# K of the middle groups in one load, into two of three neighbouring pages

## The chip, the cores and the metric

The kernel runs on one core of a Trainium2 chip. Its five engines have instruction streams of their own and meet through semaphores: TensorE (PE in the profile, its weight loads PEld), VectorE (DVE), ScalarE (ACT), GpSimd (POOL) and SyncE (SP, which here issues every transfer). Transfers are carried by 16 DMA engines. The metric is the device time of one execution in microseconds (us); lower is better.

## The reference

One token is decoded through a gated mix of two branches: attention over a cache of 32,768 positions, and a small SwiGLU layer.

```python
B, Sq, D = 1, 1, 512
Hq, Hkv, Sk, Dh = 32, 8, 32768, 128          # 4 query heads share one of 8 groups of K and V
q = (x @ wq).reshape(B, Sq, Hq, Dh).transpose(0, 2, 1, 3)
scores = jnp.einsum("bhqd,bhkd->bhqk", q, k) * (Dh ** -0.5)
p = softmax(scores, axis=-1)
a = jnp.einsum("bhqk,bhkd->bhqd", p, v) ... @ wo
b = (silu(B_x @ w_gate) * (B_x @ w_up)) @ w_down           # F = 1792
g = sigmoid((A_x * gate_w).sum(-1, keepdims=True))
return g * a + (1 - g) * b
```

All tensors are bf16. K and V are 8.4 MB for each of the 8 groups, 134 MB together; all weights add some 14 MB.

## The kernel before, in words

A loop goes round G = 8 times, once for each group. A partition p holds 256 neighbouring positions of a group, 64 KB of K and as many of V. They lie in pages of 32 KB per partition (`page`, five of them): K's first 128 positions per partition (half b = 0) in page 0, its second 128 (b = 1) in page 1, V in pages 2 and 3. Page 3 first holds w_gate and w_up, page 4 first wq and at the end wo.

**K on TensorE** (`emit_k`, for each half). A half is cut into UPP = 8 units of 16 positions. `emit_fill` (L309) transposes a unit with eight fp32 transposes into one of two PSUM tiles `pst`; VectorE copies it to one of four tiles `ktT` (L635); `emit_scores` (L321) multiplies it with the queries, 16 small matmuls into the half's PSUM bank `ps_sc`. Unit u's fill stands ahead of the scores of unit u - 2 (LAG = 2). A fill waits until the copy two units back has emptied its PSUM tile, and scores wait for their own copy. Each half begins with two fills and ends with two scores, so the pipeline empties between the halves. After a half VectorE takes its maximum (L640).

**Softmax and V.** VectorE joins both maxima (L642), TensorE transposes (L343), VectorE reduces and makes a diagonal (L650, L654), and TensorE spreads it over the partitions (L347). ScalarE makes the bias of it (`nbias`, L516) and runs eight Exps (L523), four per half. Ahead of L516 it loads a function table in every turn. TensorE multiplies with V (L362), then sums the denominators (L374) and, from ScalarE's copy `acc` (L532), the parts of the output (L383). That is the end of a turn for TensorE.

**SP's queue.** SP issues wq, the two small rows, w_gate and w_up. Then, for each group in order, K's half 0, K's half 1, V; then w_down (`wd`) and wo in five pieces. A half of K waits until TensorE has filled the same half of the group before (`sem_fill`, `load_k`, L261 and L263); V waits until TensorE has finished V of the group before (`sem_v_free`, L269 and L274). Every K load has rows of 32 KB. V has one load with 64 KB rows, but for the last group, which is loaded in halves (L280). V's single load raises one semaphore; POOL waits on it and raises the second half's (L253 to L255).

**The end.** After the loop TensorE multiplies w_down (`emit_end`), VectorE makes the transposed output `O2` of all groups (L678, L685, L687), and TensorE multiplies with wo piece by piece as it lands (`emit_wo`: 24 rows as strips, L214, 8 rows as L225). ScalarE copies the strips' sum (L697), TensorE adds it, VectorE casts the result (L699) and SP stores it (L701).

On TensorE all of this is one instruction stream: group g + 1's fills stand behind group g's reduce, and the end behind group 7's reduce.

Of the kernel before, what the change touches and what calls it, by code (L numbers as in the profile page):

```python
# [5 lines left out]
ACT = mybir.ActivationFunctionType  # L6
ALU = mybir.AluOpType
AX = mybir.AxisListType
BF16 = mybir.dt.bfloat16
# [3 lines left out]
def bass_gated_mix__gqa_block_cached__swiglu_ffn__decode_kernel(  # L13
# [52 lines left out]
    assert RQ * HPG <= 32 and RQ * DH == 512  # L66
    assert QT == 2 and QN == 512 and F % (NSTRIP * FC) == 0 and FS <= 512

    PG_K = (0, 1)
    PG_V = 2  # L70
    PG_F = 3
    PG_X = 4
    NPG = 5

    with ExitStack() as es:
        def S_(name):
# [56 lines left out]
        def T(name, shape, dt):  # L133
            return es.enter_context(nc.sbuf_tensor(name, shape, dt))
# [25 lines left out]
        diag = T("diag", [HPG, HPG], FP32)  # L160
        nbias = T("nbias", [128, HPG], FP32)
        esum = T("esum", [128, NB, HPG], FP32)
        esum2 = T("esum2", [128, HPG], FP32)
        acc = T("acc", [128, RQ, DH], FP32)
        rS = T("rS", [128, HPG], FP32)
# [7 lines left out]
        def P(name, shape, dt):  # L173
            return es.enter_context(nc.psum_tensor(name, shape, dt))

        ps_sc = [P(f"ps_sc{i}", [128, 512], FP32) for i in range(NB)]
# [30 lines left out]
        wq_v = page[:, PG_X, 0 : KC * H * DH].rearrange("p (c n) -> p c n", c=KC)  # L207
# [40 lines left out]
        with nc.Block("main") as block:  # L248
            @block.gpsimd
            def _(pool):  # L250
                pool.memset(ones_f[:, :], 1.0).then_inc(sem_ones, 1)
                pool.memset(ones_bf[:, :], 1.0).then_inc(sem_ones, 1)
                for g in range(G - 1):  # L253
                    pool.wait_ge(sem_v[0], 16 * (g + 1))
                    pool.sem_inc(sem_v[1], 16)  # L255

            @block.sync
            def _(sp):
                def load_k(g, b):
                    if g:  # L260
                        sp.wait_ge(sem_fill, UPG * (g - 1) + UPP * (b + 1))  # L261
                    src = A_k_cache[0, g, :, :].rearrange("(p b r) d -> p b r d", b=NB, r=R)
                    sp.dma_start(  # L263
                        page[:, PG_K[b], :].rearrange("p (r d) -> p r d", d=DH), src[:, b, :, :]
                    ).then_inc(sem_k[b], 16)

                def load_v(g):
                    if g:
                        sp.wait_ge(sem_v_free, STEP * g)  # L269
                    else:  # L270
                        sp.wait_ge(sem_pe_h, 1)
                    src = A_v_cache[0, g, :, :].rearrange("(p b r) d -> p b r d", b=NB, r=R)
                    if g < G - 1:
                        sp.dma_start(  # L274
                            vpage.rearrange("p b r d -> p (b r d)"),
                            src.rearrange("p b r d -> p (b r d)"),
                        ).then_inc(sem_v[0], 16)
                    else:
                        for b in range(NB):
                            sp.dma_start(vpage[:, b, :, :], src[:, b, :, :]).then_inc(  # L280
                                sem_v[b], 16
                            )

                sp.dma_start(wq_v, A_wq.rearrange("(p c) n -> p c n", c=KC)).then_inc(sem_q, 16)
                sp.dma_start(x_row[0:1, :], A_x[0, :, :]).then_inc(sem_ld_x, 16)
                sp.dma_start(gw_row[0:1, :], gate_w.unsqueeze(0)).then_inc(sem_ld_g, 16)
                for w, src in enumerate((B_w_gate, B_w_up)):
                    sp.dma_start(  # L288
                        wgu[:, w, :, :], src.rearrange("(p c) f -> p c f", c=KC)
                    ).then_inc(sem_f, 16)  # L290
                for g in range(G):
                    for b in range(NB):
                        load_k(g, b)
                    load_v(g)
                sp.dma_start(  # L295
                    wd[:, :, :], B_w_down.rearrange("(p j) n -> p j n", j=FC)
                ).then_inc(sem_ld_wd, 16)
                src = A_wo.rearrange("(p j) n -> p j n", j=WOJ)
                for k, s in enumerate(sem_wo):
                    a, b = WO_CUTS[k], WO_CUTS[k + 1]  # L300
                    sp.dma_start(wo_v[:, a:b, :], src[:, a:b, :]).then_inc(s, 16)  # L301

            @block.tensor
            def _(pe):
                def emit_fill(b, u):
                    kv = page[:, PG_K[b], :].bitcast(FP32)
                    for k in range(RPU):
                        n = u * RPU + k
                        ins = pe.transpose(  # L309
                            pst[u % NST][:, k * 128 : (k + 1) * 128],  # L310
                            kv[:, n * 128 : (n + 1) * 128],
                            ident_f[:, :],
                        )
                    ins.then_inc(sem_fill, 1)
# [12 lines left out]
                            )  # L327
                    return ins

                def emit_k(i, b):  # L330
                    pe.wait_ge(sem_k[b], i + 16)
                    for u in range(UPP + LAG):
                        if u >= LAG:
                            pe.wait_ge(sem_cp, i + (UPP * b + u - LAG + 1))
                        if u < UPP:
                            emit_fill(b, u)
                        if u >= LAG:
                            ins = emit_scores(b, u - LAG)
                    ins.then_inc(sem_sc, UPP)

                def emit_max(i):
                    pe.wait_ge(sem_pm, i + STEP)
# [49 lines left out]
                def emit_start():  # L392
# [84 lines left out]
                    pe.wait_ge(sem_ps0, 1)  # L477

                    with pe.Fori(0, G * STEP, STEP) as i:
                        for b in range(NB):  # L480
                            emit_k(i, b)
                        emit_max(i)
                        emit_v(i)
                        emit_reduce(i)
# [20 lines left out]
            @block.scalar  # L505
            def _(act):
                act.wait_ge(sem_pe_g, 1)
                act.activation(
                    g_col[:, :], ps_m[:, M_G0 : M_G0 + 1], ACT.Sigmoid
                ).then_inc(sem_act_g, 1)  # L510
                act.wait_ge(sem_pe_h, 1)
                act.activation(sg, pst[1][:, 0:FS], ACT.Sigmoid).then_inc(sem_act_sg, 1)

                with act.Fori(0, G * STEP, STEP) as i:
                    act.wait_ge(sem_b, i + STEP)
                    act.activation(  # L516
                        nbias[:, :], ps_m[:, M_B0 : M_B0 + HPG], ACT.Copy, scale=-SCALE
                    ).then_inc(sem_nbias, STEP)
# [12 lines left out]
                    act.wait_ge(sem_v_free, i + STEP)  # L531
                    act.activation(part, ps_o[:, :], ACT.Copy).then_inc(sem_acc, STEP)  # L532

            @block.vector
            def _(dve):
# [93 lines left out]
                dve.tensor_copy(tT[:, :], ps_m[:, M_T0 : M_T0 + FC]).then_inc(sem_dve_tT, 1)  # L629

                with dve.Fori(0, G * STEP, STEP) as i:
                    for b in range(NB):
                        for u in range(UPP):
                            dve.wait_ge(sem_fill, i + (UPP * b + u + 1))
                            dve.tensor_copy(  # L635
                                ktT[:, u % NKT, :], pst[u % NST][:, :].bitcast(BF16)
                            ).then_inc(sem_cp, 1)
                        dve.wait_ge(sem_sc, i + UPP * (b + 1))
                        sc = ps_sc[b][:, :].rearrange("p (t h) -> p h t", h=HPG)
                        dve.tensor_reduce(pmaxf[:, b, :], sc, AX.X, ALU.max).then_inc(sem_d, 1)  # L640
# [93 lines left out]
```

## Time and profile before

| | |
|---|---|
| median of 3 runs | 351.64 us (351.43 to 351.78) |
| the profiled execution | 351.67 us, span 350.4 us |
| mean granted TensorE clock | 0.864 |
| TensorE busy | 254.6 us (73%) |
| weight loads | 209.2 us (60%) |
| VectorE busy | 192.1 us (55%) |
| ScalarE busy | 42.9 us (12%) |
| read from HBM | 148.11 MB, 423 GB/s over the span |

Busy time is the time in which an engine has an instruction running; it says nothing on whether anybody waits for it. In the groups of instructions a line gives the source line, the engine, the operation, output and inputs, and how often it ran. In the timeline the first two columns are the start and the length in us, and the brackets at the end give how long the engine had been idle and what ended that. SPq is SP's queue; its rows are the issues of transfers, not their duration. The waits list the engine and line, what it waited for, the sum in us, how often, and the longest.

### The profile page before, as it was taken

How to read it: one execution, taken by the hardware profiler on the slowest of the kernel's cores; microseconds unless marked ns; L12 is line 12 of the kernel's file. 1: busy time of each engine (PE TensorE's matmuls, PEld its weight loads, DVE VectorE, ACT ScalarE, POOL GpSimd, SP SyncE). 2: the span in 40 equal slices, each digit the busy share in tenths (PEclk: the TensorE clock that was granted, in tenths of full speed). 3: DMA queues.
4: the chain of work that ended last, by engine and by line, in shares of the span. 5: the costliest groups of instructions: out<-in, count | busy, mean ns of one | idle time of the engine just before them, and what ended most of it. 6: DMA issues, size and time to landing. Idle time of an engine off the chain costs nothing.

```text
span 350.4 us, 8660 instructions
## 1 busy us (share of the span) xinstructions
PE 254.6 (73%) x3871; PEld 209.2 (60%) x3871; DVE 192.1 (55%) x242; ACT 42.9 (12%) x156; POOL 0.4 (0%) x6
## 2 busy tenths in 40 slices
PE   1443986688857994898858993798768893798574
PEld 1113985288725984398726991498627891498431
DVE  4243986068803885068804892088705891198500
ACT  1000000400050002300050005000050005000130
POOL 0000000000000000000000000000000000000000
PEclk9965999699968997689969997889859995899878
DMA  8999999999989999999999999999999999999995
GB/s 337 408 451 419 477 443 384 423 430 456 464 385 417 456 426 430 423 464 434 434 404 419 464 449 400 423 449 434 434 419 419 464 434 415 423 426 434 420 423 205
DMA packets 4914, 148.21 MB, mean 423 GB/s; under 512 B 554, under 2 KB 556, under 8 KB 940
## 3 DMA queue, kind: packets, MB, share of 16 engines
q1 hardware_dynamic: 4908, 148.12, 98.4%
q8 instruction: 5, 0.08, 0.1%
q14 instruction: 1, 0.01, 0.0%
HBM read 148.11 MB, written 0.00 MB: 423 GB/s over the span
## 4 chain that ended last, share of the span: by engine, by line
DMA 69%; PE 25%; DVE 3%; SPq 1%; ACT 1%; issue 1%; DVEq 0%; ACTq 0%
DMA page<-in_A_k_cache_dram 56%; PE pst L309 18%; DMA page<-in_A_wo_dram 12%; PE ps_sc L321 5%; DVE ktT L635 2%; PE ps_o L362 2%; SPq L301 0%; ACT ET L523 0%; ACT L516 0%; SPq L288 0%; SPq L280 0%; DVE pmaxf L640 0%; PE ps_m L347 0%; SPq L295 0%; PE ps_sc L225 0%
## 5 line engine op out<-in xcount | busy, mean ns | idle before, releaser
L635 DVE COPY ktT<-pst 128x2048 bf16<-128x2048 bf16 x128 | 155.4, 1223 | 31.1 <-PE pst L309 23.4
L309 PE MATMUL pst<-ident_f,page 128*128 128x128 f32 x1024 | 140.5, 286 | 15.6 <-DMA page<-in_A_k_cache_dram 10.3
L309 PEld LDWEIGHTS pst<-ident_f,page 128*128 128x128 f32 x1024 | 115.9, 146 | 19.8 <-DMA page<-in_A_k_cache_dram 11.0
L321 PE MATMUL ps_sc<-qcur,ktT 128*128 128x8 bf16 x2048 | 67.8, 166 | 8.6 <-DVE ktT L635 8.6
L321 PEld LDWEIGHTS ps_sc<-qcur,ktT 128*128 128x128 bf16 x2048 | 66.7, 97 | 11.2 <-DVE ktT L635 10.0
L362 PE MATMUL ps_o<-page,ET 128*16 128x512 bf16 x512 | 43.6, 515 | 27.1 <-ACT ET L523 27.1
L362 PEld LDWEIGHTS ps_o<-page,ET 128*16 128x16 bf16 x512 | 15.8, 113 | 51.5 <-issue 36.4
L516 ACT ACT_TABLE_LOAD x8 | 10.3, 1283 | 239.0 <-PE ps_m L347 239.0
L658 DVE TENSOR_TENSOR esum<-esum 128x4 f32<-128x4 f32 x8 | 1.3, 164 | 42.7 <-ACT ET L523 42.7
L523 ACT ACTIVATE ET<-ps_sc,nbias 128x128 bf16<-128x128 f32 x64 | 23.9, 562 | 0.7
L662 DVE RECIPROCAL rS<-ps_sc 128x4 f32<-128x4 f32 x8 | 1.5, 182 | 34.2 <-PE ps_sc L374 34.2
L523 ACT ACTIVATION_READ_ACCUMULATOR ET<-ps_sc,nbias 128x1 f32 x64 | 18.6, 290 | 0.0
L640 DVE TENSOR_REDUCE pmaxf<-ps_sc 128x4 f32<-128x512 f32 x16 | 11.1, 692 | 10.4 <-PE ps_sc L321 10.4
L383 PE MATMUL ps_m<-sel,acc 128*128 128x4 f32 x64 | 8.4, 255 | 3.6 <-ACT acc L532 3.6
L383 PEld LDWEIGHTS ps_m<-sel,acc 128*128 128x128 f32 x64 | 7.7, 191 | 4.3 <-ACT acc L532 4.3
L343 PE MATMUL ps_m<-ident_f,pmax 128*4 128x128 f32 x8 | 2.5, 308 | 9.1 <-DVE pmax L642 9.1
L532 ACT ACTIVATE acc<-ps_o 128x512 f32<-128x512 f32 x8 | 4.8, 597 | 34.5 <-PE ps_o L362 34.5
L347 PE MATMUL ps_m<-diag,ones_f 4*128 4x4 f32 x16 | 3.6, 294 | 6.3 <-DVE diag L654 6.3
L347 PEld LDWEIGHTS ps_m<-diag,ones_f 4*128 4x128 f32 x16 | 3.2, 244 | 8.1 <-issue 8.1
L404 PE MATMUL ps_m<-ones_bf,x_row 1*128 1x1 bf16 x4 | 0.3, 172 | 9.3 <-DMA x_row<-in_A_x_dram 9.3
L343 PEld LDWEIGHTS ps_m<-ident_f,pmax 128*4 128x4 f32 x8 | 0.6, 81 | 9.6 <-issue 9.6
L404 PEld LDWEIGHTS ps_m<-ones_bf,x_row 1*128 1x128 bf16 x4 | 0.2, 114 | 9.6 <-DMA x_row<-in_A_x_dram 9.6
(68 smaller groups left out, 53.8 us busy)
## 6 DMA issues: line engine op xcount, KB each, us to landing
page<-in_A_k_cache_dram SPq DMA_DIRECT2D x16, 4096.0 KB, 27.4
page<-in_A_v_cache_dram SPq DMA_DIRECT2D x2, 4096.0 KB, 27.3
page<-in_A_wq_dram SPq DMA_DIRECT2D x1, 4096.0 KB, 12.3
page<-in_A_wo_dram SPq DMA_DIRECT2D x1, 2048.0 KB, 40.2
page<-in_B_w_gate_dram SPq DMA_DIRECT2D x1, 1792.0 KB, 15.5
page<-in_B_w_up_dram SPq DMA_DIRECT2D x1, 1792.0 KB, 19.4
wd<-in_B_w_down_dram SPq DMA_DIRECT2D x1, 1792.0 KB, 35.8
page<-in_A_wo_dram SPq DMA_DIRECT2D x1, 1024.0 KB, 42.3
```

The source lines that it names most:

```text
L309: ins = pe.transpose(pst[u % NST][:, k * 128 : (k + 1) * 128], kv[:, n * 128 : (n + 1) * 128], ident_f[:, :],)
L321: ins = pe.matmul(ps_sc[b][:, col : col + 2 * HPG], kt[:, k, e, :], qcur[:, e, :], start=(e == 0), stop=(e == 1),)
L343: pe.transpose(ps_m[0:HPG, M_A0 : M_A0 + 128], pmax[:, :], ident_f[:, :]).then_inc(sem_t, STEP)
L347: pe.matmul(ps_m[:, M_B0 : M_B0 + HPG], ones_f[0:HPG, :], diag[:, :], start=True, stop=True,).then_inc(sem_b, STEP)
L362: ins = pe.matmul(ps_o[32 * c : 32 * c + RQ * HPG, :], ET[:, n : n + RQ, :].rearrange("p n h -> p (n h)"), vpage[:, b, k * RQ : (k + 1) * ...
L383: ins = pe.matmul(ps_m[:, M_P0 : M_P0 + HPG], acc[:, q, :], sel4[:, q * HPG : (q + 1) * HPG], start=(q == 0), stop=(q == RQ - 1),)
L516: act.activation(nbias[:, :], ps_m[:, M_B0 : M_B0 + HPG], ACT.Copy, scale=-SCALE).then_inc(sem_nbias, STEP)
L523: act.activation(ET[:, b * R : (b + 1) * R, h], sc[:, h, :], ACT.Exp, bias=nbias[:, h : h + 1], scale=SCALE, accum_out=esum[:, b, h : h + ...
L532: act.activation(part, ps_o[:, :], ACT.Copy).then_inc(sem_acc, STEP)
L635: dve.tensor_copy(ktT[:, u % NKT, :], pst[u % NST][:, :].bitcast(BF16)).then_inc(sem_cp, 1)
L640: dve.tensor_reduce(pmaxf[:, b, :], sc, AX.X, ALU.max).then_inc(sem_d, 1)
L662: dve.reciprocal(rS[:, :], ps_s).then_inc(sem_d, 1)
```

## The change

K gets three neighbouring pages, A, B and C (0, 1, 2). An even group lies in B (half 0) and C (half 1), an odd one in A (half 0) and B (half 1). So half 0 and half 1 are neighbours in both, and groups 1 to 6 are each loaded in one transfer of 64 KB rows. Groups 0 and 7 stay in two halves, page B's first. The load of a group is issued when TensorE has filled page B of the group before (one unit later for group 1). POOL relays K's semaphore as it does V's. V moves to pages 3 and 4, wq to A, wo to C; w_down's load gets a wait in front for the fills of group 6.

TensorE fills page B first in every group, then the other page. Only these second fills differ between even and odd groups: four pairs of If and Else, each with two units of fills. The fills of both pages now run on without the pipeline being emptied between them; in the second page two fills stand ahead of two scores. Page B's scores go to the first bank, and ScalarE's Exps pick the bank by a register in odd groups. The first maximum is taken after the tenth copy.

Apart from that, the bias is made by VectorE instead of ScalarE, and ScalarE runs one small Exp ahead of the loop.

```diff
-    PG_K = (0, 1)
-    PG_V = 2
-    PG_F = 3
-    PG_X = 4
+    PG_A, PG_B, PG_C = 0, 1, 2
+    PG_V = 3
+    PG_F = 4
+    PG_Q = PG_A
+    PG_X = PG_C
...
                 for g in range(G - 1):
-                    pool.wait_ge(sem_v[0], 16 * (g + 1))
-                    pool.sem_inc(sem_v[1], 16)
+                    for s in (sem_k, sem_v) if g else (sem_v,):
+                        pool.wait_ge(s[0], 16 * (g + 1))
+                        pool.sem_inc(s[1], 16)
...
-                def load_k(g, b):
+                def load_k(g):
                     if g:
-                        sp.wait_ge(sem_fill, UPG * (g - 1) + UPP * (b + 1))
+                        sp.wait_ge(sem_fill, UPG * (g - 1) + UPP + (g == 1))
+                    lo = PG_A if g % 2 else PG_B
+                    dst = page[:, lo : lo + NB, :].rearrange("p b (r d) -> p b r d", d=DH)
                     src = A_k_cache[0, g, :, :].rearrange("(p b r) d -> p b r d", b=NB, r=R)
-                    sp.dma_start(
-                        page[:, PG_K[b], :].rearrange("p (r d) -> p r d", d=DH), src[:, b, :, :]
-                    ).then_inc(sem_k[b], 16)
+                    if 0 < g < G - 1:
+                        sp.dma_start(
+                            dst.rearrange("p b r d -> p (b r d)"),
+                            src.rearrange("p b r d -> p (b r d)"),
+                        ).then_inc(sem_k[0], 16)
+                    else:
+                        for n, b in enumerate((1, 0) if g % 2 else (0, 1)):
+                            if g and n:
+                                sp.wait_ge(sem_fill, UPG * (g - 1) + UPP + 1)
+                            sp.dma_start(dst[:, b, :, :], src[:, b, :, :]).then_inc(
+                                sem_k[n], 16
+                            )
...
+                sp.wait_ge(sem_fill, UPG * (G - 1))
                 sp.dma_start(
                     wd[:, :, :], B_w_down.rearrange("(p j) n -> p j n", j=FC)
...
+                def emit_k(i):
+                    pe.wait_ge(sem_k[0], i + 16)
+                    for n in range(UPP):
+                        if n >= LAG:
+                            pe.wait_ge(sem_cp, i + (n - LAG + 1))
+                        emit_fill(PG_B, n)
+                        if n >= LAG:
+                            emit_scores(0, n - LAG)
+                    pe.wait_ge(sem_k[1], i + 16)
+                    odd = i & STEP
+                    for n in range(UPP, UPG + LAG, LAG):
+                        if n < UPG:
+                            for pg in (PG_A, PG_C):
+                                with pe.If(odd > 0) if pg == PG_A else pe.Else():
+                                    for m in range(n, n + LAG):
+                                        pe.wait_ge(sem_cp, i + (m - LAG + 1))
+                                        emit_fill(pg, m - UPP)
+                        else:
+                            pe.wait_ge(sem_cp, i + UPG)
+                        for m in range(n - LAG, n):
+                            ins = emit_scores(m // UPP, m % UPP)
+                            if m % UPP == UPP - 1:
+                                ins.then_inc(sem_sc, UPP)
...
+                act.wait_ge(sem_ones, 2)
+                act.activation(eone[:, :], ones_f[:, 0:1], ACT.Exp)
+
                 with act.Fori(0, G * STEP, STEP) as i:
-                    act.wait_ge(sem_b, i + STEP)
-                    act.activation(
-                        nbias[:, :], ps_m[:, M_B0 : M_B0 + HPG], ACT.Copy, scale=-SCALE
-                    ).then_inc(sem_nbias, STEP)
                     act.wait_ge(sem_nbias, i + STEP)
+                    odd = (i & STEP) * (R // STEP)
+                    sc = ps_all[:, :, :].rearrange("p b (t h) -> p h (b t)", h=HPG)
                     for b in range(NB):
-                        sc = ps_sc[b][:, :].rearrange("p (t h) -> p h t", h=HPG)
+                        bank = R - odd if b else odd
                         for h in range(HPG):
                             act.activation(
                                 ET[:, b * R : (b + 1) * R, h],
-                                sc[:, h, :],
+                                sc[:, h, bass.ds(bank, R)],
...
-                    for b in range(NB):
-                        for u in range(UPP):
-                            dve.wait_ge(sem_fill, i + (UPP * b + u + 1))
+                    for n in range(UPG + 1):
+                        if n < UPG:
+                            dve.wait_ge(sem_fill, i + (n + 1))
                             dve.tensor_copy(
-                                ktT[:, u % NKT, :], pst[u % NST][:, :].bitcast(BF16)
+                                ktT[:, n % NKT, :], pst[n % NST][:, :].bitcast(BF16)
                             ).then_inc(sem_cp, 1)
+                        if n not in (UPP + LAG - 1, UPG):
+                            continue
+                        b = n // UPG
                         dve.wait_ge(sem_sc, i + UPP * (b + 1))
...
+                    dve.wait_ge(sem_b, i + STEP)
+                    dve.tensor_scalar(
+                        nbias[:, :], ps_m[:, M_B0 : M_B0 + HPG], -SCALE, None, op0=ALU.mult
+                    ).then_inc(sem_nbias, STEP)
```

More of the change, by code (lines that the diff above doesn't have):

```diff
@@ L67, in bass_gated_mix__gqa_block_cached__swiglu_ffn__decode_kernel @@
     assert QT == 2 and QN == 512 and F % (NSTRIP * FC) == 0 and FS <= 512
-    PG_K = (0, 1)
-    PG_V = 2
-    PG_F = 3
-    PG_X = 4
+    PG_A, PG_B, PG_C = 0, 1, 2
[3 more added lines that the diff above has]
+    PG_X = PG_C
     NPG = 5
+    assert G % 2 == 0
     with ExitStack() as es:
@@ L162, in bass_gated_mix__gqa_block_cached__swiglu_ffn__decode_kernel @@
         esum = T("esum", [128, NB, HPG], FP32)
+        eone = T("eone", [128, 1], FP32)
         esum2 = T("esum2", [128, HPG], FP32)
@@ L174, in P @@
             return es.enter_context(nc.psum_tensor(name, shape, dt))
-        ps_sc = [P(f"ps_sc{i}", [128, 512], FP32) for i in range(NB)]
+        ps_all = P("ps_sc", [128, NB, 512], FP32)
+        ps_sc = [ps_all[:, b, :] for b in range(NB)]
         ps_o = P("ps_o", [128, 512], FP32)
@@ L206, in bass_gated_mix__gqa_block_cached__swiglu_ffn__decode_kernel @@
         vpage = page[:, PG_V : PG_V + NB, :].rearrange("p b (r d) -> p b r d", d=DH)
-        wq_v = page[:, PG_X, 0 : KC * H * DH].rearrange("p (c n) -> p c n", c=KC)
+        wq_v = page[:, PG_Q, 0 : KC * H * DH].rearrange("p (c n) -> p c n", c=KC)
         wgu = page[:, PG_F, 0 : 2 * KC * F].rearrange("p (w c f) -> p w c f", w=2, c=KC)
@@ L291, in _ @@
                 for g in range(G):
-                    for b in range(NB):
-                        load_k(g, b)
+                    load_k(g)
                     load_v(g)
+                sp.wait_ge(sem_fill, UPG * (G - 1))
                 sp.dma_start(
@@ L304, in _, with emit_fill @@
             def _(pe):
-                def emit_fill(b, u):
-                    kv = page[:, PG_K[b], :].bitcast(FP32)
+                def emit_fill(pg, u):
+                    kv = page[:, pg, :].bitcast(FP32)
                     for k in range(RPU):
@@ L328, in emit_scores @@
                     return ins
[L330 to L339, printed above, removed]
+                def emit_k(i):
[21 more added lines that the diff above has]
+                                ins.then_inc(sem_sc, UPP)
                 def emit_max(i):
@@ L479, in emit_start @@
                     with pe.Fori(0, G * STEP, STEP) as i:
-                        for b in range(NB):
-                            emit_k(i, b)
+                        emit_k(i)
                         emit_max(i)
@@ L631, in _ @@
                 with dve.Fori(0, G * STEP, STEP) as i:
-                    for b in range(NB):
-                        for u in range(UPP):
-                            dve.wait_ge(sem_fill, i + (UPP * b + u + 1))
+                    for n in range(UPG + 1):
+                        if n < UPG:
+                            dve.wait_ge(sem_fill, i + (n + 1))
                             dve.tensor_copy(
-                                ktT[:, u % NKT, :], pst[u % NST][:, :].bitcast(BF16)
+                                ktT[:, n % NKT, :], pst[n % NST][:, :].bitcast(BF16)
                             ).then_inc(sem_cp, 1)
+                        if n not in (UPP + LAG - 1, UPG):
+                            continue
+                        b = n // UPG
                         dve.wait_ge(sem_sc, i + UPP * (b + 1))
```

## The prediction

> **What bounds the kernel now.** I read the page's DMA queues first, then the timeline around the last two turns of the loop over groups, then the waits.
>
> ```profile
> q1 hardware_dynamic: 4908, 148.12, 98.4%
> q8 instruction: 5, 0.08, 0.1%
> ```
>
> The 16 DMA engines carry packets for 98.4% of the span, so up to the last weights the transfers set the time. The packet records say at what pace: a half of K (4 MB, 32 KB packets) lands 9.72 us after what was queued before it, a V (8 MB, 64 KB packets) 19.36 us after it, 38.80 us for a group. The same figure is in the first fills of groups 1 to 7, at 71.63, 110.44, 149.25, 188.04, 226.86, 265.65 and 304.46 us.
>
> ```profile
> PE pst L309 <- DMA page<-in_A_k_cache_dram: 10.3, 8, 2.9
> ```
>
> TensorE waits for K at the start of all eight groups, 10.3 us in all. Its own work on a group (first fill to the end of the reduce matmuls, L383) took 38.2, 36.9, 38.6, 38.0, 36.8, 38.4, 37.3 and 36.7 us: nearly as long as the 38.8 us of transfers. In the long ones the granted clock fell to 0.5 as the fills began. The last two groups and the end, from the timeline:
>
> ```profile
> 265.65 1.97 PE L309 MATMUL pst<-ident_f,page 128*128 128x128 f32 x16 [0.35 <-DMA page<-in_A_k_cache_dram]
> 275.75 12.12 SPq L263 DMA_DIRECT2D page<-in_A_k_cache_dram  x2
> 277.04 0.56 PE L321 MATMUL ps_sc<-qcur,ktT 128*128 128x8 bf16 x16 [0.54 <-DVE ktT L635]
> 279.84 1.09 PE L309 MATMUL pst<-ident_f,page 128*128 128x128 f32 x8 [0.45 <-DVE ktT L635]
> 289.42 0.69 DVE L640 TENSOR_REDUCE pmaxf<-ps_sc 128x4 f32<-128x512 f32 x1 [0.65 <-PE ps_sc L321]
> 292.32 1.28 ACT L516 ACT_TABLE_LOAD   x1 [28.13 <-PE ps_m L347]
> 293.61 0.17 ACT L516 ACTIVATE nbias<-ps_m 128x4 f32<-128x4 f32 x1
> 301.22 0.80 SPq L280 DMA_DIRECT2D page<-in_A_v_cache_dram  x2
> 301.94 1.05 PE L383 MATMUL ps_m<-sel,acc 128*128 128x4 f32 x8 [0.45 <-ACT acc L532]
> 304.46 1.97 PE L309 MATMUL pst<-ident_f,page 128*128 128x128 f32 x16 [1.47 <-DMA page<-in_A_k_cache_dram]
> ...
> 340.07 1.05 PE L383 MATMUL ps_m<-sel,acc 128*128 128x4 f32 x8 [0.45 <-ACT acc L532]
> 342.26 0.19 DVE L687 CAST O<-ps_m 128x32 bf16<-128x32 f32 x1 [0.30 <-PE ps_m L493]
> 346.00 0.60 ACT L697 ACTIVATE acc<-ps_sc 128x512 f32<-128x512 f32 x1 [5.98 <-PE ps_sc L214]
> 347.93 0.38 PE L225 MATMUL ps_sc<-page,O 128*1 128x128 bf16 x8 [0.29 <-DMA page<-in_A_wo_dram]
> 348.36 0.29 DVE L699 CAST res_row<-ps_sc 128x128 bf16<-128x128 f32 x1 [5.91 <-PE ps_sc L225]
> ```
>
> Three things are to be seen. Group 7 begins at 304.46, when its first half of K is there, 1.47 us after group 6 has left TensorE (302.99). The end hangs on the last piece of wo (347.93). And the arithmetic is only a little ahead of it: O2 is ready at 342.45, and without waits on wo what follows would take 1.03 (16 strips), 0.60 (8 strips), 0.05 + 0.60 + 0.18 (ScalarE's copy and its handoff), 0.39, 0.40 and 0.38 us: TensorE would end at 346.1 instead of 348.31. So the **slack of the end is 2.2 us**.
>
> **The sum's base.** The profiled execution took 351.67 us, its span 350.4; the median of the runs is 351.64. I add to 351.67; the 0.03 us between them is dropped.
>
> **The change, part by part.**
>
> *The loads.* For groups 1 to 6 two rows of 32 KB become one of 64 KB. Two 32 KB packets take 2 x 1222 ns (median 1216) and one of 64 KB 2425 (2421): 11 to 19 ns, times 8 packets per engine, times 6 groups, 0.5 to 0.9 us. The landings give 2 x 9.72 - 19.36 = 0.08 us a group, 0.5 us; I take that. A group's transfers then take 38.72 us.
>
> *When TensorE may begin.* This is the large term. Before, a group starts when the first half of K has landed; now all of it must. Group 6's second half landed at 274.89 us (one half, 9.72, after the first). With 0.5 us gained it lands at 274.4, and its first fill, 0.49 us behind the landing as in each group of before, stands at **274.9 instead of 265.65**. In groups 1 to 5 this delay costs nothing while the transfers stay gapless, because each group is late by the same 9.2 us. Group 7 is still loaded in halves (landings near 303.5 and 313.2), but TensorE is then in group 6, and there is no later group to make it up.
>
> *SP's queue.* K's load is issued at the first half's end as before, now whole, so nothing moves later; V's load behind it waits for the V matmuls as before. V(g+1) must be moving before K(g+1) has landed. V matmuls end some 1.8 us before the reduce, so with the length of a group found below at 34.8 us after the first fill; the first issue of the program took 1.0 us to its first packet: 35.8. K(g+1) lands 38.2 us after the first fill on the slowest DMA engine, 36.1 on the fastest (landings spread 2.1 us). It holds by 0.3 us on the fastest and 2.4 on the slowest, which is the one that counts. The wait put ahead of wd is met by group 6's last fill, before V(7) is issued. POOL's added relays sit beside 8 units of fills that need no second half.
>
> *The second page's order on TensorE.* Before: the last fill of the first half ends at 275.73, the third fill of the second half starts at 279.84, 4.11 us, as two scores wait for a copy of 1.23 us. Now: a score 0.38, two fills at 0.94, two scores, 3.0 us: 1.1 us saved. The next six fills stay at 7.7 us: a pair needs 2 x 0.94 + 2 x 0.38 = 2.64 on TensorE against 2 x 1.27 on VectorE, and the first max (0.69 us), now between the copies, costs about 0.4 once. At the end both last scores wait for the last copy and a copy is still queued: 3.2 us from last fill to max instead of 2.6, 0.6 lost. Sum: 0.4 us saved without branches.
>
> *Four If/Else pairs.* The trace of before shows no branch between fills. Lower end: 0, where TensorE's sequencer is ahead. Nearest row: the loop's own jump back, with at most 0.18 us between group 3's reduce (149.07) and its next fill (149.25), which waited for K as well. I take 0.15 a pair, half of it hidden behind the added max in the second: 0.3 to 0.5 us a group, 0.4. Upper end: an instruction packet of 16 KB, 1.07 us in the records, at each pair, 4.3 us a group.
>
> [...]
>
> *Exp's table and the bias.* The bias matmul ends at 292.25, the first Exp starts at 293.88: table load 1.28 and copy 0.17 lie between. With the load ahead of the loop and VectorE scaling (its small operations take 0.16) some 0.3 us remain: 1.3 saved. If the load stays in the loop, nothing is saved, so 0 to 1.3; I take 1.3, since L512's Sigmoid after L508's shows no second load. The Exps' register-given bank: 0 to 0.1 us for each of the four ahead of V (the register-given copy L645 takes 0.17, like its neighbours), taken as 0.1 in all.
>
> A group thus gets shorter by 0.4 - 0.4 + 1.3 - 0.1 = **1.2 us**, between -3.9 and 1.7.
>
> **The sum.** Group 6: TensorE now idles some 2 us ahead of it. With 1.9 and 2.1 us of idle, groups 2 and 5 took 38.6 and 38.4; with 0.4 to 1.5 others took 36.7 to 37.3. I take 37.8 - 1.2 = 36.6: its reduce ends at 311.5. Group 7 follows without a wait, 0.2 later; 36.7 to 38.0 (group 3, 0.2 us of idle) less 1.2, taken as 35.9: 347.6 instead of 341.12, 6.5 us later. Less the slack of 2.2: **+4.3 us, 355.9**. V(7) and wo have then landed (by 347), so they cost nothing, and the 0.5 us of faster loads is no longer seen at the end except in where group 6 starts.
>
> The range of this case: both groups short (36.8, 36.7) and 1.7 saved in each, delay 4.0, +1.8, 353.5; both long (38.5, 38.0) with the table load left in and 0.6 of branches (1.5 us longer than my middle), delay 10.4, +8.2, 359.9.
>
> **Rivals.**
>
> *TensorE becomes the bound in every group.* If a pair costs 1 us, a group takes 37.7 + 1.7 = 39.4 us and 0.2 between groups; from group 1's start at 81.3 the reduce of group 7 ends at 81.3 + 7 x 39.6 = 358.5, 17.4 late, +15.2: 366.9. It decides from 0.7 us a pair, where a group passes 38.7. For it: TensorE runs with only 2 us spare, and V's issue is within 0.3 us of leaving the fastest DMA engine idle. Against it: five instruction packets in the whole run, though the loop goes round eight times, so its body is not fetched again. Chance 0.12.
>
> [...]
>
> *The end is not reached: not slower.* If two groups together get 6.1 us shorter than 74.5 (some 3 us each instead of 1.2), group 7 is done in time for the last wo, and only the faster packets show: 351.67 - 0.5 = 351.2. The place is the last two groups, the price 0, and it decides from 3 us saved a group. For it: a busier TensorE might be granted its full clock in both groups (36.7 each), which is worth 1.2 of it. Against: after that 2.4 a group would still have to come from where I find 1.2. Chance 0.11, of which 0.04 passes 0.2% with packets at the upper price (0.9 us).
>
> *The rows bring nothing:* 64 KB packets with K's source as slow as 32 KB. That moves my forecast by 0.5 us and lies in its range.
>
> **How the numbers follow.** Forecast 0.77, TensorE-bound 0.12, not slower 0.11. A measurement here tells some 0.2% (0.7 us) from no change. Faster 0.04, same 0.08 (the not-slower case and a sliver of the forecast's lower end), slower 0.88. The forecast's own range is 353.5 to 359.9; to hold 8 in 10 the stated one reaches down to the not-slower case, 351.0 to 360.2, and leaves out the TensorE-bound one and what of the forecast lies beyond its bounds.
>
> **What would show it.** First fills of groups 1 to 6 at 81.3 and each 38.7 us on; group 6's at 274.9; group 7's with no wait on K, near 311.7; V matmuls of group 7 near 345; no wait on wo in the last rows; DMA done some 7 us before the end; ScalarE with two table loads. I am wrong if group 7 starts before 309 (the groups got much shorter), if first fills lie over 39 us apart (TensorE or late V loads bound), or if group 1 starts its fills near 72 us.

## The result, and the profile after

The changed kernel takes **356.95 us** in the median of four runs (356.3 to 357.69) against 351.71 before: a ratio of 1.0151, with a 95% interval of 1.013 to 1.0172. It is slower by 5.2 us. The profiled execution is the longest of the four: 357.69 us, with a span of 356.1.

The page's DMA queues, to be compared with 98.4% before:

```profile
q1 hardware_dynamic: 4044, 148.12, 97.4%
q8 instruction: 5, 0.08, 0.1%
```

The same 148.12 MB come in 864 packets fewer, over a longer span. The instruction packets are still five, so the larger loop body is not fetched again in each turn. The waits, which count the engine's idle time in all, how often, and the longest:

```profile
PE pst L325 <- DMA page<-in_A_k_cache_dram: 28.9, 7, 11.4
```

TensorE's wait for K has grown from 10.3 to 28.9 us. The longest, 11.4, is in front of group 1, which now starts when its whole K has landed. And it is seven waits, not eight: group 7 doesn't wait. The timeline of the last two groups and the end:

```profile
277.19 4.50 PE L325 MATMUL pst<-ident_f,page 128*128 128x128 f32 x24 [2.19 <-DMA page<-in_A_k_cache_dram]
...
290.50 0.94 PE L337 MATMUL ps_sc<-qcur,ktT 128*128 128x8 bf16 x32
291.31 1.94 PE L325 MATMUL pst<-ident_f,page 128*128 128x128 f32 x16
...
301.13 0.69 DVE L672 TENSOR_REDUCE pmaxf<-ps_sc 128x4 f32<-128x512 f32 x1 [1.05 <-PE ps_sc L337]
303.39 0.55 PE L376 MATMUL ps_m<-diag,ones_f 4*128 4x4 f32 x2 [0.79 <-DVE diag L686]
304.06 0.16 DVE L690 TENSOR_SCALAR nbias<-ps_m 128x4 f32<-128x4 f32 x1 [0.81 <-PE ps_m L376]
304.43 0.55 ACT L552 ACTIVATE ET<-ps_sc,nbias 128x128 bf16 x1 [30.53 <-DVE nbias L690]
312.63 0.80 SPq L296 DMA_DIRECT2D page<-in_A_v_cache_dram  x2
313.34 1.06 PE L412 MATMUL ps_m<-sel,acc 128*128 128x4 f32 x8 [0.45 <-ACT acc L561]
314.26 1.94 PE L325 MATMUL pst<-ident_f,page 128*128 128x128 f32 x16
...
348.39 1.05 PE L412 MATMUL ps_m<-sel,acc 128*128 128x4 f32 x8 [0.45 <-ACT acc L561]
350.56 0.19 DVE L723 CAST O<-ps_m 128x32 bf16<-128x32 f32 x1 [0.29 <-PE ps_m L521]
353.68 0.41 PE L229 MATMUL ps_sc<-page,O 128*1 128x128 bf16 x16
354.12 0.29 DVE L735 CAST res_row<-ps_sc 128x128 bf16<-128x128 f32 x1 [3.37 <-PE ps_sc L229]
```

Group 6 starts at 277.19 us instead of 265.65, group 7 right behind it at 314.26 instead of 304.46, without a wait. The last rows of wo (353.68) wait for no transfer either: the trace's packet records have the last of wo landed at 351.06. So the end is now set by TensorE's last two groups, as forecast. The bias is made in 0.16 us by VectorE, and no table load stands in the loop any more.

One thing was not forecast, and it is one that the prediction named as a sign of being wrong (first fills over 39 us apart). First fills are 38.72 us apart from group 1 to 2 (81.21, 119.93) and from 3 to 4 (159.78, 198.51), but 39.85 and 39.97 us from 2 to 3 and from 4 to 5 (238.48). V(2)'s issue, and twelve microseconds around it and around V(3)'s at 153.80, from the view by windows (the last two columns are the DMA engines' share and GB/s):

```profile
116.11 0.33 SPq L290 DMA_DIRECT2D page<-in_A_v_cache_dram  x1
114.00:126.00 12.00, 9.50 (x115) 8.00 (x107) 4.46 (x7) 0.60 (x1) 0.00 (x0) 0.86 0.97 382
152.00:164.00 12.00, 7.33 (x66) 6.04 (x55) 2.30 (x5) 0.60 (x1) 0.00 (x0) 0.76 1.01 437
```

By the packet records the K in front of V(2) lands from 117.54 us (fastest DMA engine) to 119.44 (slowest), and V(2) 20.6 us later instead of 19.36: its landing loses 1.3 us, although V was issued 1.4 us before the first engine ran dry. Every engine lost something here. Five had no packet for 4.8 us in all; the last of them got its first one 3.2 us after the issue. The other eleven went on from K to V at once, but their first two packets took together 0.7 to 1.3 us longer than twice 2.42. Single first packets took up to 4.0 us. The landings of V(4) and V(6) lose 1.3 and 1.2 us, though at V(4) some engines lose less than 0.1 us; the landing here is that of the slowest engine. V(3) and V(5), issued 3.6 and 2.9 us before, lose nothing.

### The profile page after: what moved, and what is told of

It reads as the page before. It is cut to its first block, busy times and chain, and to the rows that moved or that the text cites. A ratio compares the mean times of both kernels' runs of the same rounds, so it can differ in the third digit from the quotient of the medians.

```text
span 356.1 us, 8774 instructions
## 1 busy us (share of the span) xinstructions
PE 260.4 (73%) x3871; PEld 215.7 (61%) x3871; DVE 190.0 (53%) x250; ACT 32.9 (9%) x142; POOL 0.4 (0%) x6
## 3 DMA queue, kind: packets, MB, share of 16 engines
q1 hardware_dynamic: 4044, 148.12, 97.4%
## 5 line engine op out<-in xcount | busy, mean ns | idle before, releaser
L664 DVE COPY ktT<-pst 128x2048 bf16<-128x2048 bf16 x128 | 153.5, 1221 | 55.0 <-PE pst L325 50.6
L325 PE MATMUL pst<-ident_f,page 128*128 128x128 f32 x1024 | 145.1, 296 | 29.4 <-DMA page<-in_A_k_cache_dram 28.9
L325 PEld LDWEIGHTS pst<-ident_f,page 128*128 128x128 f32 x1024 | 123.7, 152 | 33.6 <-DMA page<-in_A_k_cache_dram 29.5
L337 PE MATMUL ps_sc<-qcur,ktT 128*128 128x8 bf16 x2048 | 64.3, 166 | 7.5 <-DVE ktT L664 6.4
L337 PEld LDWEIGHTS ps_sc<-qcur,ktT 128*128 128x128 bf16 x2048 | 63.9, 97 | 9.3 <-DVE ktT L664 7.1
L391 PE MATMUL ps_o<-page,ET 128*16 128x512 bf16 x512 | 42.4, 504 | 17.0 <-ACT ET L552 17.0
L552 ACT ACTIVATE ET<-ps_sc,nbias 128x128 bf16 x64 | 24.1, 562 | 260.2 <-DVE nbias L690 260.2
L391 PEld LDWEIGHTS ps_o<-page,ET 128*16 128x16 bf16 x512 | 14.5, 112 | 41.6 <-issue 18.3
L552 ACT ACTIVATION_READ_ACCUMULATOR ET<-ps_sc,nbias 128x1 f32 x64 | 18.6, 291 | 0.0
L376 PE MATMUL ps_m<-diag,ones_f 4*128 4x4 f32 x16 | 4.4, 340 | 6.3 <-DVE diag L686 6.3
L704 DVE TENSOR_SCALAR oTw<-ps_m 128x4 f32 x8 | 1.3, 162 | 8.4 <-PE ps_m L412 8.4
## 6 DMA issues: line engine op xcount, KB each, us to landing
page<-in_A_wq_dram SPq DMA_DIRECT2D x1, 4096.0 KB, 12.2
```

What stands on the lines that cost most here:

```text
L325: ins = pe.transpose(pst[u % NST][:, k * 128 : (k + 1) * 128], kv[:, n * 128 : (n + 1) * 128], ident_f[:, :],)
L337: ins = pe.matmul(ps_sc[b][:, col : col + 2 * HPG], kt[:, k, e, :], qcur[:, e, :], start=(e == 0), stop=(e == 1),)
L376: pe.matmul(ps_m[:, M_B0 : M_B0 + HPG], ones_f[0:HPG, :], diag[:, :], start=True, stop=True,).then_inc(sem_b, STEP)
L391: ins = pe.matmul(ps_o[32 * c : 32 * c + RQ * HPG, :], ET[:, n : n + RQ, :].rearrange("p n h -> p (n h)"), vpage[:, b, k * RQ : (k + 1) * ...
L552: act.activation(ET[:, b * R : (b + 1) * R, h], sc[:, h, bass.ds(bank, R)], ACT.Exp, bias=nbias[:, h : h + 1], scale=SCALE, accum_out=esum ...
L664: dve.tensor_copy(ktT[:, n % NKT, :], pst[n % NST][:, :].bitcast(BF16)).then_inc(sem_cp, 1)
```

## The experiments

Two causes stand against each other, and two rivals. **Late start**: K is usable only when whole, so the last two groups end late (the forecast). **Late V issue**: V comes too close to the end of the queue, which delays every later landing. The rivals: TensorE's new order and its branches, and the 64 KB rows themselves.

### K in halves for every group

K always comes in two loads, page B's half first, and POOL relays V alone:

```diff
-                    if 0 < g < G - 1:
+                    if False:
...
-                    for s in (sem_k, sem_v) if g else (sem_v,):
-                        pool.wait_ge(s[0], 16 * (g + 1))
-                        pool.sem_inc(s[1], 16)
+                    pool.wait_ge(sem_v[0], 16 * (g + 1))
+                    pool.sem_inc(sem_v[1], 16)
```

> The changed kernel, but K of every group comes in two loads of 32 KB rows, page B's half first, both issued where the one load was. Late start (K usable only when whole): first fills go back to 71.6, 110.4, ... 304.5 us, 9.7 us ahead of the changed kernel's, V is issued some 10 us before the queue ends, group 7's reduce ends by 339.7 and the end hangs on wo again: 351.7 us, within 0.5. TensorE's new order and the If/Else as the cause: the slowdown stays, 356 or more. Slow 64 KB rows as the cause: about 351.7 too, but then a whole K would have to take over 2 x 9.72 us in the changed kernel, which its landings (19.36 where nothing stalls) don't show.

Measured: 351.68 us, a ratio to the kernel before of 1.0003 (0.9994 to 1.0012). Its timeline and wait:

```profile
PE pst L324 <- DMA page<-in_A_k_cache_dram: 15.6, 8, 2.8
```

```profile
265.68 4.38 PE L324 MATMUL pst<-ident_f,page 128*128 128x128 f32 x24 [1.27 <-DMA page<-in_A_k_cache_dram]
304.49 5.38 PE L324 MATMUL pst<-ident_f,page 128*128 128x128 f32 x24 [1.90 <-DMA page<-in_A_k_cache_dram]
...
347.95 0.38 PE L229 MATMUL ps_sc<-page,O 128*1 128x128 bf16 x8 [0.27 <-DMA page<-in_A_wo_dram]
```

Groups 6 and 7 start within 0.03 us of the kernel before and the end hangs on wo again. All of the slowdown hangs on K coming whole; three pages, If/Else, two fills ahead of two scores and the bias on VectorE cost nothing. The end's slack doesn't hide a cost either, as groups 1 to 7 took 36.8 us on TensorE in the mean, against 37.5 in the kernel before. TensorE's new order falls as a cause. The expectation missed in one place: group 7's reduce ended at 341.1 us, not by 339.7, as the fills of its page B took 11.95 us instead of 10.1, at a granted clock of 0.56 in their first 6 us. The 64 KB rows as such fall too, by the landings: a whole K that follows without a loss lands 19.36 us after what was ahead of it (80.72 after 61.36 us in the changed kernel), two halves need 19.44.

### Only group 6 in halves, only V in halves, and both

Group 6 in halves, in POOL's relay and in the load:

```diff
-                    for s in (sem_k, sem_v) if g else (sem_v,):
+                    for s in (sem_k, sem_v) if 0 < g < G - 2 else (sem_v,):
...
-                    if 0 < g < G - 1:
+                    if 0 < g < G - 2:
```

> The changed kernel, but group 6's K too comes in halves, so TensorE may start it 9.7 us earlier. Late start: group 5 leaves TensorE only at 275.0, so group 6 starts there instead of at 277.2, both last groups run without idling, the reduce of group 7 ends near 346.5 instead of 349.4, V(7) is issued without a stall: 354.3 us, within 1. If the last groups don't matter: 357.

V in halves, each issued when its own half's matmuls are done (a semaphore more, raised behind half 0; POOL then relays K alone):

```diff
                 def load_v(g):
-                    if g:
-                        sp.wait_ge(sem_v_free, STEP * g)
-                    else:
+                    if not g:
                         sp.wait_ge(sem_pe_h, 1)
...
+                    for b in range(NB):
+                        if g:
+                            sp.wait_ge(sem_v_free if b else sem_v_half, STEP * g)
+                        sp.dma_start(vpage[:, b, :, :], src[:, b, :, :]).then_inc(sem_v[b], 16)
...
-                    ins.then_inc(sem_v_free, STEP)
+                        ins.then_inc(sem_v_free if b else sem_v_half, STEP)
```

> The changed kernel, but V of every group is loaded in halves, each issued when its own half's matmuls are done, the first some 2.5 us earlier than before. Late V issue as the cause of the 1.3 us lost in front of V(2), V(4), V(6): these go to zero, group 6 starts near 275.1 instead of 277.2 and the rest of the delay stays, as it comes from the last two groups: 355.0 us, within 0.7. If the lost 1.3 us have another cause (the 64 KB rows of K): 357.

> The two edits before together: group 6's K in halves, and every V in halves. If late start in the last groups and late V issue are the whole of it, group 6 starts when group 5 has left TensorE, near 272.9, the reduce of group 7 ends near 344 and the end is within 0.5 us of hanging on wo: 352.0 us, within 0.8. If TensorE's order or the branches have a part: 354 or more.

Measured: 352.63 us with group 6 in halves (1.0046, 1.0023 to 1.0069), 354.71 with V in halves (1.0092, 1.0062 to 1.0122), 351.81 with both (1.0009, 1.0000 to 1.0018). First fills of groups 6 and 7 and the last reduce, with V in halves:

```profile
275.38 4.51 PE L320 MATMUL pst<-ident_f,page 128*128 128x128 f32 x24 [2.11 <-DMA page<-in_A_k_cache_dram]
310.85 1.94 PE L320 MATMUL pst<-ident_f,page 128*128 128x128 f32 x16
345.92 1.05 PE L407 MATMUL ps_m<-sel,acc 128*128 128x4 f32 x8 [0.45 <-ACT acc L556]
```

and with both:

```profile
273.64 1.95 PE L320 MATMUL pst<-ident_f,page 128*128 128x128 f32 x16
308.67 1.94 PE L320 MATMUL pst<-ident_f,page 128*128 128x128 f32 x16
342.40 1.06 PE L407 MATMUL ps_m<-sel,acc 128*128 128x4 f32 x8 [0.45 <-ACT acc L556]
```

With V issued earlier all first fills are 38.80 us apart and group 6 starts 1.8 us earlier: that is the late V issue, 2.2 us of the 5.2 in the medians. The 3 us that remain are the late start. In the other order the shares differ: group 6 in halves alone takes 4.3 us away, and V in halves 0.8 more; with group 6 in halves the Vs also lost less. Both edits together take the two causes away and all but 0.2 us of the slowdown. The expectation for group 6 alone missed by 1.7 us: in its profile V(2) and V(4) lost 0.5 and 0.7 us instead of 1.3 each, so group 5 started and ended over a microsecond earlier and group 6 began at 273.5, not at 275.0. Its runs spread from 351.75 to 355.35 us.

### How early an issue has to come

The kernel before, with V issued only after n fills of its group, and nothing else changed; n = 1, 3 and 5:

```diff
-                        sp.wait_ge(sem_v_free, STEP * g)
+                        sp.wait_ge(sem_fill, UPG * g + n)
```

> The kernel before, with V issued after the first fill of its group, some 111.6 us for V(2), 6 us ahead of the fastest DMA engine's end of the K in front of it. By either theory nothing is lost: 351.7 us, within 0.5, V lands 19.36 us after K.

> The kernel before, but V of a group is issued only when TensorE has done the first 3 fills of that group, some 114.3 us for V(2), while the K in front of it lands from 117.6 (fastest DMA engine) to 119.7 us (slowest): 3 us ahead of the fastest. Nothing else changes. If an issue has to come some 3 us before the queue runs dry, the loss is between 0 and 1.3 us a V, up to 9 us in all. If only a really empty queue costs (about 1 us of latency): nothing, 351.7 us.

> The kernel before, with V issued after the fifth fill of its group, some 117.2 us for V(2), 0.4 us ahead of the fastest DMA engine's end of the K in front of it and 2.5 ahead of the slowest's. If an issue has to come some 3 us ahead, each V loses 1.3 to 2.5 us: V lands 20.7 to 21.9 us after K, some 9 to 17 us for seven, 361 to 369 us. If only an empty queue costs: the slowest engine never runs dry, V lands within 0.3 us of 19.36 after K, 352 us.

Measured: 351.66 us (1.0004, 0.9992 to 1.0016), 351.85 (1.0006, 0.9996 to 1.0016) and 360.47 (two runs; 1.0256, 1.0212 to 1.03). From the packet records, the time from V's issue to the fastest engine's end of the K in front, and by how much V then landed later than 19.36 us behind that K (on the slowest engine), for the Vs that came in one load, of these three and of the other kernels here:

| issued ahead, us | of which kernels | lost, us |
|---|---|---|
| 5.3 to 6.2 | n = 1, all six | 0.0 |
| 2.5 to 3.9 | n = 3, five; n = 5, one; changed kernel, V(3) and V(5); three of its variants | 0.0 |
| 1.4 to 2.4 | n = 3, one (0.0 at 2.0); changed kernel, V(2) (1.3 at 1.4); variants (0.9 at 2.1, 0.2 at 2.3) | 0.0 to 1.3 |
| under 1.4 | n = 5, five; changed kernel, V(4) and V(6) (1.3 and 1.2); variants | 0.3 to 2.6 |

From 2.5 us ahead nothing was lost in any of them, under 1.4 something always; between, both occur. With n = 5 the engines carry little at all around V(2), issued at 120.23 us, here 1.6 us behind the fastest engine's end:

```profile
118.00:124.00 6.00, 6.00 (x105) 5.94 (x104) 5.52 (x5) 0.00 (x0) 0.00 (x0) 1.00 0.64 235
```

Three microseconds ahead cost nothing, the lower end of what was expected. For n = 5 the expected 361 to 369 us were just missed, since V(5) lost 0.3 us and V(6), issued 2.5 us ahead, nothing. The other theory, that only an empty queue costs, is wrong: at n = 5 the slowest engine still had 2.2 to 3.0 us of K to carry at V(1), V(3) and V(4), and yet these landed 1.2 to 2.6 us late; with the engines' ends compared in order, first with first and so on, each was at least 0.5 us late. Part of the loss is time in which engines had no packet, as at V(2) of the changed kernel. Why engines that went on at once had slower packets the records don't show; that stays open.

### The bias back on ScalarE, and the bias alone

The changed kernel with the bias of the Exps (L552) from ScalarE again and no Exp ahead of the loop:

```diff
+                    act.wait_ge(sem_b, i + STEP)
+                    act.activation(
+                        nbias[:, :], ps_m[:, M_B0 : M_B0 + HPG], ACT.Copy, scale=-SCALE
+                    ).then_inc(sem_nbias, STEP)
...
-                    dve.wait_ge(sem_b, i + STEP)
-                    dve.tensor_scalar(
-                        nbias[:, :], ps_m[:, M_B0 : M_B0 + HPG], -SCALE, None, op0=ALU.mult
-                    ).then_inc(sem_nbias, STEP)
```

> The changed kernel with the bias back on ScalarE and no Exp ahead of the loop, as in the kernel before; all else as changed. Late start and late V issue: a group gets 1.25 us longer on TensorE, so V is issued 1.25 us closer to the end of the queue in every group; where the changed kernel lost 1.3 us (V(2), V(4), V(6)) it is some 2.5, where it lost nothing about 1.3, and the last two groups add 1.25 each: group 6 starts near 282, 365 us, within 3. If the bias only matters in the last two groups: 359.5.

and the opposite edit in the kernel before:

> The kernel before with only the bias moved to VectorE and the Exp ahead of the loop. A group gets 1.25 us shorter on TensorE (36.9 to 35.7 in the short ones), but the transfers set the end and group 7 already waits for K and wo: 351.7 us, within 0.4, group 7's reduce 1.3 us earlier near 339.8. If the arithmetic of the end were on the path: 350.4.

Measured: 359.56 us (1.0217, 1.0184 to 1.025) and 351.57 (0.9993, 0.9984 to 1.0003). In the changed kernel the bias on VectorE is worth 2.6 us in the medians: from the last score to the first V matmul the last two groups took 5.95 and 6.26 us instead of 4.99 and 4.88, 2.3 us together. In the kernel before it is worth nothing that can be measured, as the end hangs on wo:

```profile
347.92 0.28 PE L226 MATMUL ps_sc<-page,O 128*1 128x128 bf16 x8 [0.36 <-DMA page<-in_A_wo_dram]
```

The second expectation named 351.7 and holds for the time; but the reduce of group 7 ended at 341.9, not 339.8, as its first page's fills took 12.2 us instead of 10.1, at a granted clock of 0.50 where it had been 1.00 before (means from 304 to 310 us). The first named 365 and was wrong: V(2) lost 1.9 us, but V(3), V(4) and V(5) together only 0.4, and group 6 started at 277.28, as in the changed kernel. The reason is in the sum: V(g + 1) is issued when group g's V matmuls are done, some 34 us after group g starts in the changed kernel and 35 to 37 here, and the K in front of it lands 38.7 us after K(g) plus whatever V(g) lost. A loss of one V therefore puts the next one's issue further ahead of the queue's end by as much. Losses don't add up with the length of the groups. In the changed kernel they alternate: V(3) was issued 2.1 us further ahead than V(2), of which 1.1 is V(2)'s loss and 1.0 the shorter group 2 (35.6 us after 36.7), and so it goes on with V(4) to V(6).

### Twice the branches

```diff
-                            for pg in (PG_A, PG_C):
-                                with pe.If(odd > 0) if pg == PG_A else pe.Else():
-                                    for m in range(n, n + LAG):
+                            for m in range(n, n + LAG):
+                                for pg in (PG_A, PG_C):
+                                    with pe.If(odd > 0) if pg == PG_A else pe.Else():
                                         pe.wait_ge(sem_cp, i + (m - LAG + 1))
                                         emit_fill(pg, m - UPP)
```

> The changed kernel with an If/Else pair round each of the 8 units of the second page instead of each two, twice the branches, the order of the work unchanged. In the changed kernel the fills of the second page end 10.3 us after those of the first, with no visible gap at a branch; if branches hide behind the matmuls that are queued, that stays 10.3 us and the time 357.0 within 1. If a pair costs 0.15 us and more: 10.9 us or more, 1.2 us for the last two groups and later V issues: 359 or more.

Measured: 356.61 us (1.0143, 1.0126 to 1.016), the changed kernel's time. Its timeline at the first two pairs of units in group 6's second page:

```profile
288.15 2.17 PE L325 MATMUL pst<-ident_f,page 128*128 128x128 f32 x16
290.15 0.94 PE L337 MATMUL ps_sc<-qcur,ktT 128*128 128x8 bf16 x32
290.96 1.95 PE L325 MATMUL pst<-ident_f,page 128*128 128x128 f32 x16
```

From scores to the next fills it takes 0.81 us, as with half the branches (290.50 to 291.31), and from the end of the first page's fills to the end of the second's 10.30 us in both. Doubling the branches does not lengthen this stretch: nothing of them shows on TensorE's path.

## Why the prediction was right

The forecast was 355.9 us, the median is 356.95; the direction and the large term hold. One term was far too small, and smaller ones made up for part of it. That the forecast lies within 1.1 us of the median is in part luck. The sum below is that of the profiled execution, which at 357.69 us is 0.7 above the median.

**When TensorE may begin** was the large term and holds: nine microseconds of lateness that cost groups 1 to 5 nothing and show at the end. With K in halves everywhere they vanish, with group 6's K and V's issue mended they vanish too.

**SP's queue** is the step that failed. It took the 1.0 us from issue to first packet for what V's issue needs and found it held by 0.3 us on the fastest engine and 2.4 on the slowest, "which is the one that counts". The 1.3 us that it left between issue and the fastest engine's end were right (1.42 at V(2)); the need was too small. In these runs an issue 2.5 us before the *fastest* engine ran dry lost nothing, and under 1.4 us each V in one load landed late, by 0.3 to 2.6 us. Missing was 2.3 us at group 6's start: 277.19 instead of 274.9. By these losses (4.6 us in all, 0.8 of them at V(7), issued 1.1 us ahead) the last of wo landed at 351.06 us and not by 347, 5.0 us before the end of the span and not 7; TensorE came to it later still.

**The loads**: 0.08 us a group as worked out (19.36 against 19.44).

**The second page's order and the branches**: the second page's fills take 10.30 us against 11.78 before, where 10.7 without and 11.1 with branches were forecast (the working names 0.4 us more for the first maximum, but leaves it out of its sum: 1.1 less 0.4 and 0.6 is 0.1, not 0.4; the runs show no such cost); what is lost at the end of a group is 0.65 us (2.53 against 1.88 from the last fill to the last score), as forecast. The branches' 0.4 us is 0. No run shows the 0.6 us a group either that the upper end of the range counts for them: with eight pairs a group, as with four, the second page's fills took 10.30 us, so nothing of the branches reaches the path here.

**Exp's table and the bias**: 1.05 to 1.26 us saved from last score to first V matmul (4.88 to 4.99 against 5.93 to 6.24), forecast 1.3 less 0.1.

**A group's length.** These parts save 1.9 to 2.1 us a group where 1.2 was forecast, but the mean of groups 1 to 7 fell by 1.3 only. The fills of page B, whose work is the same in both kernels, took 11.3 us in the mean instead of 10.5: TensorE now idles 2.0 to 11.4 us ahead of groups 1 to 6, and the granted clock over these fills was 0.77 to 0.85 there, where it had been 0.84 to 1.00 before. The prediction allowed for this in group 6 alone.

**The sum.** Group 7 took 35.2 us (forecast 35.9) and its fills began 0.1 us before the reduce of group 6 had ended (forecast 0.2 after). Group 6 took 37.2 (forecast 36.6): its V matmuls ran 6.50 us, against 4.98 to 5.88 before, at a granted clock of 0.5 for most of it. From the reduce to the end of TensorE it was 4.65 us where 5.0 were worked out. In all: 347.6 + 2.3 + 0.6 - 0.3 - 0.7 = 349.5 for the last reduce, measured 349.44. The upper bound of the forecast's own range was added up too low: groups of 38.5 and 38.0 us, 0.3 longer each, from 274.9 on end near 352.2, a delay of 11.1 and not 10.4 us, 360.6 and not 359.9.

**The rivals.** TensorE did not become the bound in every group: the groups stayed at 35.2 to 37.3 us, under 38.7, and the branches cost nothing. First fills over 39 us apart came from the V loads, the other cause that the prediction gave for that sign. A packet fetched at each pair, the upper end of what the branches could cost, doesn't show: five instruction packets came in the whole run, as before, all of them ahead of 70 us. The not-slower case needed 3 us a group; the shortest group went from 36.7 to 35.2, the mean of groups 1 to 7 from 37.5 to 36.2.

Nothing tried beats the kernel before by more than can be told apart. What could be had from 64 KB rows of K is 0.08 us in each of six groups, 0.5 us or 0.14%, and only where a group's lateness is paid back before the end and V is still issued 2.5 us ahead.

## What to carry to other kernels

A larger load could be used here only when all of it had landed: group 1's first fill came at 81.21 us instead of 71.63. In this loop, bound by transfers, that cost nothing in every turn but the last two, and there a part of it showed at the end (some 3 of 9.2 us). So work out the last two turns before anything else. Merging the loads also moved what the later work issues (here V) towards the end of the queue: V(2) was issued 1.4 us before the fastest engine's end of K, where it had been 10.8. So check how long before the *fastest* DMA engine's last packet each issue comes (in these runs 2.5 us cost nothing, under 1.4 us always something), not only whether the queue is ever empty. And keep the last turns in small pieces even if the middle is merged.

## What the runs showed of the hardware

- In the changed kernel an 8 MB load issued 0.7 to 1.4 us before the first of the 16 DMA engines had finished the load ahead landed 1.2 to 1.3 us late. At V(2) also the engines with over 3 us left lost 0.7 us or more, and first packets took up to 4.0 us instead of 2.42. Issued 2.5 us or more ahead it cost nothing in any run.
- From the issue to the first packet of the first engine it took 1.0 us (V(2) at n = 5: issued at 120.23, first packet at 121.20); an idle engine got its own up to 3.2 us after the issue (V(2) of the changed kernel).
- In the changed kernel, where V's issue hangs on the group before, such losses limited themselves: V(2) landed 1.3 us late and delayed the K behind it, which is 1.1 of the 2.1 us by which V(3) was issued further ahead, and V(3) lost nothing. With n = 5, where V hangs on its own group's fills, V(1) to V(5) all lost, 0.3 to 2.6 us.
- If/Else in TensorE's stream: with four and with eight pairs a group the second page's fills took the same 10.30 us.
